# One transformer block on one core: a hand-written order of all operations replaced by another order of the same operations

## The chip, the cores and the metric

The kernel runs on one core of one Trainium2 chip. The metric is the device time of one execution in microseconds, the median over several runs. The core has five engines that run side by side, each of them through its own list of instructions in a fixed order: TensorE (PE), VectorE (DVE), ScalarE (ACT), GpSimd (POOL) and SyncE (SP). SP does no arithmetic here. It issues nearly all DMA transfers, one after the other; ACT issues the first two. An engine whose next instruction is not ready waits, and everything behind that instruction on the same engine waits with it.

## The reference: what is computed

A conditioning vector `c` gives shifts, scales and gates through `silu(c) @ w_mod`, six blocks of 512. A layer norm of x, scaled and shifted by the first two blocks, goes through sliding dilated attention; its output, multiplied by the third block, is added to x. A second layer norm, scaled and shifted by the next two blocks, goes through a gated GELU network; its output, multiplied by the sixth block, is added again. S is 2048, the width 512, there are 32 heads of 16, the window holds 8 keys at distances 0, 2, ... 14, and the hidden width is 1792. The two cores of it:

```python
idx = pos[:, None] - off[None, :]          # off = arange(8) * 2
logits = jnp.einsum('bhsd,bhswd->bhsw', q, kg) * scale
logits = jnp.where(mask[None, None, :, :], logits, -1000000000.0)
attn = _softmax(logits, axis=-1)
o = jnp.einsum('bhsw,bhswd->bhsd', attn, vg)
...
g = jnp.einsum('bsd,df->bsf', x, w_gate)
u = jnp.einsum('bsd,df->bsf', x, w_up)
h = _gelu(g) * u                            # then h @ w_down
```

## The kernel before, in words

The sequence is cut into four groups of 512 positions, each of four chunks of 128. Every step of the kernel is an `Op` with the engine that it goes to, a function that emits its instructions, the names of the ops that must come first, and the name that it fires when it is emitted. The ops stand in 123 generators, here called threads. Each thread gives its ops in a fixed order of its own: one thread for the matmuls of the query, key and value projection of group 0, one for the VectorE products of group 0, and so on. 26 such threads serve each group; others serve the loads, the conditioning vector, the warming up of TensorE and the scaling of the weights.

The order in which the threads are interleaved is written out by hand, as a list of thread numbers called `ORDER` at the top of the file:

```python
def run(self):
    nxt = [next(g, None) for g in self.threads]
    for i in ORDER:
        op = nxt[i]
        ...
        op.fn()
        ...
        nxt[i] = next(self.threads[i], None)
```

So `ORDER` alone decides which instruction stands behind which on each engine. The numbers that an `Op` carries as its duration are not used for anything when the kernel is built.

The threads that matter for the change, with the names of their ops and the lines that issue instructions (a trailing number is the group, then the head block or chunk):

- Warming up (thread 10): 15 matmuls on zeros, L202. They compute nothing that is used.
- Conditioning (thread 9): the activation `s4` of `c` on ACT (L315), its transposition `scp` on PE (L320), a copy back (`scT`, L324), a tiny exponential whose purpose is its table load (`pre`, L326), and two products with `w_mod`, `mp1` and `mp0` (L286), whose evictions give scale and shift of the first norm (L294, L291). Each of these products waits for its own 512 KB load, `wm1` and `wm0` (L223).
- Norms: statistics on DVE (`st`, L395; `ag`, L401), or on ACT for some chunks (`sa`, L378; `sq`, L384); the variance made ready (`vd`, L415, from DVE; `va`, L420, from ACT); the power -0.5 on POOL (`rs`, L426); the normalised chunks `x0` to `x3` on DVE (L435). LN1.g is the first norm of group g, LN2.g the second. LN1.0 is done in two halves of two chunks. Then come transposes, on PE (`th0` and `th1` at L472 for LN1.0, L449 for LN1.1, LN1.2 and LN2.0) or by DMA (L455), and the evictions with scale and shift (L487 on ACT; for LN1.0 L505 on ACT and L503 on DVE).
- Projections (`qp`, L536 and L554), evicted by ACT (L568, L570, L572).
- Attention of a group: `pq` multiplies queries with shifted keys on DVE (four ops, L617); `lp` sums over the head width on PE (L631); softmax on DVE and ACT (L643 to L675), for groups 2 and 3 behind a tiny exponential (`pre.2`, `pre.3`, L682) that loads its table; the probabilities go to memory and come back replicated (`est`, L687, and `pt`, L694, on SP); the values go to memory (`vst`, L591) and come back shifted (`V4`, four loads, L599); `pv` multiplies on DVE (four ops, L706); `o` sums on PE (L720); `oT` evicts on ACT (L731); `x1p` is the output projection (L741), and `x1` adds it to x on DVE (L750).
- Network of a group: 14 pairs of gate and up products on PE (`g` and `u`, L771), GELU and copy on ACT (`gl`, L803; `ub`, L810), their product on DVE (`hh`, L821), the down projection on PE (`y`, L783; `yl`, L794 for the very last chunk), the sum with x on DVE (`ot`, L828; L835 for the last) and the stores (L843, L852).
- Gates: the third block of the conditioning scales the weights `wo` on DVE (`woS`, L361), the sixth the weights of the down projection, in seven pieces (`WdS0` to `WdS6`, L356). Both need the gate spread over all partitions in one tile `gB`. That goes through memory: a store of 1 KB (`gst`, L298) and a load that replicates it (`ga` for `woS`, `gb` for `WdS`, L303). Blocks four and five pass through memory too (L305). The weights of the down projection come in four loads (`Wd0` to `Wd3`, L243). `Wd0` uses the buffer of the value weights again, so it has to wait until the last value projection of group 3 has read them.

SP's order is therefore part of `ORDER` too: a transfer that must wait there holds all transfers listed behind it.

Of the kernel before, what the change touches and what calls it, by code (L numbers as in the profile page):

```python
# [18 lines left out]
    1, 26, 2, 10, 0, 10, 2, 1, 2, 0, 2, 10, 10, 2, 10, 0, 10, 9, 10, 2, 9, 20, 9, 10, 20, 10, 18, 20, 10, 21,  # L19
    10, 18, 20, 10, 20, 2, 21, 20, 21, 10, 21, 10, 10, 21, 20, 20, 2, 9, 9, 9, 9, 21, 22, 9, 21, 10, 17, 23, 22,  # L20
    17, 3, 23, 24, 17, 24, 24, 11, 17, 23, 24, 17, 24, 24, 24, 44, 46, 2, 24, 24, 2, 46, 25, 25, 2, 46, 46, 24,
    25, 2, 46, 46, 44, 24, 2, 46, 25, 46, 24, 46, 25, 28, 24, 25, 4, 3, 24, 25, 70, 46, 24, 72, 70, 46, 24, 25,
    46, 46, 25, 28, 48, 25, 24, 49, 48, 49, 24, 49, 28, 49, 11, 29, 25, 29, 25, 50, 72, 27, 27, 11, 96, 5, 50,
    28, 96, 3, 50, 70, 51, 29, 70, 27, 72, 52, 72, 29, 98, 96, 27, 72, 30, 50, 51, 30, 5, 96, 50, 72, 51, 30,
    72, 51, 50, 51, 72, 30, 50, 98, 72, 72, 72, 96, 12, 13, 30, 74, 12, 51, 6, 50, 96, 98, 53, 30, 53, 50, 51,
    98, 51, 75, 30, 98, 50, 74, 75, 54, 31, 50, 27, 13, 75, 7, 50, 75, 51, 98, 78, 31, 55, 51, 98, 31, 76, 98,
    98, 54, 100, 76, 77, 76, 77, 76, 77, 16, 76, 4, 27, 77, 4, 32, 76, 4, 77, 6, 76, 77, 4, 51, 76, 4, 32, 77,
    4, 101, 76, 77, 76, 101, 32, 101, 33, 77, 33, 55, 101, 76, 77, 32, 51, 102, 77, 34, 76, 34, 7, 33, 54, 79,
    79, 4, 53, 33, 34, 4, 103, 102, 53, 34, 53, 102, 54, 53, 35, 35, 36, 55, 55, 36, 19, 7, 35, 56, 6, 19, 104,
    35, 19, 36, 77, 103, 102, 36, 37, 19, 102, 37, 103, 37, 102, 37, 103, 37, 37, 102, 56, 103, 37, 103, 102,  # L30
    103, 37, 56, 37, 102, 37, 37, 103, 56, 14, 103, 38, 14, 102, 39, 56, 38, 39, 102, 56, 39, 102, 39, 80, 57,
    103, 40, 4, 103, 8, 103, 40, 80, 40, 57, 57, 41, 40, 41, 40, 8, 41, 42, 41, 4, 40, 4, 41, 42, 4, 105, 40,
# [872 lines left out]
```

## Time and profile before

| | |
|---|---|
| median of three runs | 236.47 us (236.15 to 236.91) |
| span of the profiled execution | 234.1 us |
| TensorE busy | 228.9 us, 98% of the span |
| VectorE busy | 167.5 us, 72% |
| ScalarE busy | 148.4 us, 63% |
| GpSimd busy | 24.7 us, 11% |
| DMA moved | 30.42 MB |

The span runs from the first to the last instruction of the profiled execution. The runs are 2.4 us longer than that span, which is work outside the kernel's own instructions. Times within the profile are microseconds from the start of the span. Row heads read: start, length, engine, line, operation, output and inputs; "x8" means that eight instructions stand in one row; what stands in square brackets is the time that the engine sat idle ahead of the row and what released it. PE rows whose pieces overlap the next row are normal, since the ends of pipelined matmuls are modelled.

### The profile page before, as it was taken

How to read it: one execution, taken by the hardware profiler on the slowest of the kernel's cores; microseconds unless marked ns; L12 is line 12 of the kernel's file. 1: busy time of each engine (PE TensorE's matmuls, PEld its weight loads, DVE VectorE, ACT ScalarE, POOL GpSimd, SP SyncE). 2: the span in 40 equal slices, each digit the busy share in tenths (PEclk: the TensorE clock that was granted, in tenths of full speed). 3: DMA queues.
4: the chain of work that ended last, by engine and by line, in shares of the span. 5: the costliest groups of instructions: out<-in, count | busy, mean ns of one | idle time of the engine just before them, and what ended most of it. 6: DMA issues, size and time to landing. Idle time of an engine off the chain costs nothing.

```text
span 234.1 us, 3657 instructions
## 1 busy us (share of the span) xinstructions
PE 228.9 (98%) x1382; PEld 107.2 (46%) x1382; DVE 167.5 (72%) x240; ACT 148.4 (63%) x282; POOL 24.7 (11%) x37
## 2 busy tenths in 40 slices
PE   7899999999999999999999999999999999999995
PEld 2755454444544444444444444444444444444443
DVE  4889999999998999989999989916642122123222
ACT  4999996968995749928556961563568721466400
POOL 3210230892100000100000010000100000000000
PEclk9999999999999999999999999999999999999999
DMA  6998869999368280054404634100071001000011
GB/s 214 385 332 295 244 224 221 301 329 408 159 188 235 97 276 3 1 115 134 114 0 128 243 91 97 40 0 22 0 71 45 0 22 42 6 0 1 21 48 45
DMA packets 30313, 30.42 MB, mean 130 GB/s; under 512 B 14936, under 2 KB 26200, under 8 KB 30296
## 3 DMA queue, kind: packets, MB, share of 16 engines
q1 hardware_dynamic: 29760, 29.67, 41.3%
q10 hardware_dynamic: 536, 0.53, 0.6%
q8 instruction: 11, 0.18, 0.3%
q14 instruction: 6, 0.05, 0.1%
HBM read 22.78 MB, written 5.31 MB: 120 GB/s over the span
## 4 chain that ended last, share of the span: by engine, by line
PE 84%; DVE 9%; DMA 3%; ACT 1%; SPq 1%; issue 0%
PE g_ps L771 21%; PE u_ps L771 21%; PE y_ps L783 19%; PE qkv_ps L554 9%; PE x_ps L741 6%; DVE pq L617 5%; PE o_ps L720 3%; DMA x<-in_A_x_dram 3%; PE LTp L631 2%; PE y_ps L794 1%; DVE xn L435 1%; DVE st L395 1%; ACT qT L568 1%; DVE mx L648 1%; DVE LTp L654 1%; DVE e L675 1%
## 5 line engine op out<-in xcount | busy, mean ns | idle before, releaser
L771 PE MATMUL g_ps<-h,Wg 128*128 128x512 bf16 x224 | 57.5, 379 | 0.0
L771 PE MATMUL u_ps<-h,Wu 128*128 128x512 bf16 x224 | 57.5, 379 | 0.0
L803 ACT ACTIVATE gl<-g_ps 128x512 bf16<-128x512 f32 x56 | 33.8, 605 | 24.3 <-PE g_ps L771 23.4
L783 PE MATMUL y_ps<-Wd,hht 128*128 128x512 bf16 x210 | 47.0, 379 | 0.0
L821 DVE TENSOR_TENSOR hht<-gl,ub 128x512 bf16<-128x512 bf16 x56 | 23.2, 420 | 31.8 <-ACT ub L810 31.6
L810 ACT CAST ub<-u_ps 128x512 bf16<-128x512 f32 x56 | 33.0, 592 | 17.1 <-PE u_ps L771 17.1
L554 PE MATMUL qkv_ps<-hT,wqkv 128*128 128x512 bf16 x184 | 42.0, 380 | 0.2 <-ACT gR L349 0.2
L617 DVE TENSOR_TENSOR pq<-qT,kT 128x4096 bf16<-128x4096 bf16 x16 | 36.3, 2284 | 0.3 <-ACT kT L570 0.3
L706 DVE TENSOR_TENSOR pv<-PT,V 128x4096 bf16<-128x4096 bf16 x16 | 36.0, 2285 | 0.2 <-PE LTp L631 0.2
L771 PEld LDWEIGHTS <-Wg 128*128 128x128 bf16 x224 | 21.7, 98 | 27.2 <-issue 1.7
L771 PEld LDWEIGHTS <-Wu 128*128 128x128 bf16 x224 | 21.8, 98 | 26.8 <-issue 0.8
L783 PEld LDWEIGHTS <-hht 128*128 128x128 bf16 x210 | 20.4, 98 | 25.2 <-issue 0.8
L554 PEld LDWEIGHTS <-wqkv 128*128 128x128 bf16 x184 | 20.2, 114 | 18.8 <-issue 2.4
L426 POOL TENSOR_TENSOR rstd<-rstd,neghalf 128x4 f32<-128x4 f32 (+1 forms) x9 | 8.7, 971 | 122.3 <-DVE rstd L415 68.7
L828 DVE TENSOR_TENSOR ot<-y_ps,x 128x512 bf16<-128x512 f32 x15 | 10.2, 686 | 15.9 <-PE y_ps L783 15.9
L750 DVE TENSOR_TENSOR x<-x_ps,x 128x512 bf16<-128x512 f32 x16 | 10.8, 684 | 7.1 <-PE x_ps L741 7.1
L741 PE MATMUL x_ps<-woP,oT 128*128 128x512 bf16 x64 | 15.3, 379 | 0.0
L395 DVE BATCH_NORM_STATS2 st<-x 128x6 f32<-128x512 bf16 x19 | 12.5, 678 | 2.5 <-DMA x<-in_A_x_dram 2.5
L487 ACT ACTIVATE h<-h,modT,scl 128x512 bf16<-128x512 bf16 x12 | 9.0, 808 | 8.1 <-DMA h<-xn 8.1
L587 POOL COPY vh<-vT 128x64 bf16<-128x64 bf16 x3 | 12.0, 3992 | 16.7 <-ACT vT L572 16.7
L731 ACT CAST oT<-o_ps 128x512 bf16<-128x512 f32 x16 | 9.2, 600 | 6.6 <-PE o_ps L720 6.6
L378 ACT ACTIVATE gl<-x 128x512 bf16<-128x512 bf16 x13 | 8.3, 650 | 6.8 <-DVE x L750 6.0
(77 smaller groups left out, 186.8 us busy)
## 6 DMA issues: line engine op xcount, KB each, us to landing
V<-vscr SPq DMA_DIRECT2D x16, 526.0 KB, 6.7
wm<-in_w_mod_dram SPq DMA_DIRECT2D x5, 512.0 KB, 8.5
vscr<-vT SPq DMA_DIRECT2D x4, 528.0 KB, 7.4
out_dram<-ot SPq DMA_DIRECT2D x15, 128.0 KB, 1.7
Wg<-in_B_w_gate_dram SPq DMA_DIRECT2D x4, 448.0 KB
Wu<-in_B_w_up_dram SPq DMA_DIRECT2D x4, 448.0 KB, 7.6
wqkv<-in_A_wqkv_dram SPq DMA_DIRECT2D x3, 512.0 KB, 7.1
x<-in_A_x_dram SPq DMA_DIRECT2D x3, 512.0 KB, 8.0
```

The source lines that it names most:

```text
L395: nc.vector.bn_stats(out=k["st", c4][:], in_=src()[:, c4, :])
L554: nc.tensor.matmul(ps[:], lhsT=wqkv[blk][:, dt, j::4], rhs=B["hT", sg][:, :, dt, :], start=(dt == 0), stop=(dt == DT - 1))
L587: yield Op("POOL", 0.2, lambda: nc.gpsimd.tensor_copy(out=vh[:], in_=B["vT", sg][:, :, SG:VR]), after=[f"qkv.{sg}.2.3"], fire=f"vh.{sg}")
L617: nc.vector.tensor_tensor(out=pq[:], in0=_ap(B["qT", sg][:, j, :], [[0, W], [1, SG]]), in1=_ap(kT[:, j, sg * SG + 2:sg * SG + 2 + SG], [[2 ...
L706: nc.vector.tensor_tensor(out=t[:], in0=_ap(B["PT", sg][:, 0, :], [[SG, 2], [0, 4], [1, SG]]), in1=_ap(v[:, j, 0, :], [[8, 2], [VR, 4], [1 ...
L741: nc.tensor.matmul(ps[:], lhsT=B["oT", sg][:, j, c4 * P:(c4 + 1) * P], rhs=woP[:, j, :], start=(j == 0), stop=(j == 3))
L750: nc.vector.tensor_tensor(out=x[:, c4, :], in0=B["x1ps", sg, c4][:], in1=x[:, c4, :], op=ALU.add)
L771: nc.tensor.matmul(ps[:], lhsT=Wt[:, dt, ft * P:(ft + 1) * P], rhs=B["h2T", sg][:, :, dt, :], start=(dt == 0), stop=(dt == DT - 1))
L783: nc.tensor.matmul(ps[:], lhsT=B["hh", sg, ft][:, c4 * P:(c4 + 1) * P], rhs=B["Wd", ft // 4][:, ft % 4, :], start=(ft == 0), stop=(ft == F ...
L803: nc.scalar.activation(out=gl[:], in_=B["g", sg, ft][:], func=ACT.Gelu_apprx_tanh)
L810: nc.scalar.copy(out=ub[:], in_=B["u", sg, ft][:])
L821: nc.vector.tensor_tensor(out=hh[:], in0=B["gl", sg, ft][:], in1=B["ub", sg, ft][:], op=ALU.mult)
```

## The change

Only `ORDER` changes. The ops, their functions, buffers, shapes and data are the same, and so is the order within each thread. The whole list is replaced; its numbers tell a reader little. Its first line, for instance (10 is the warming up, 26 the zeroing of a margin, 2 the loads on SP, 20 the statistics of group 0):

```diff
 ORDER = [
-    1, 26, 2, 10, 0, 10, 2, 1, 2, 0, 2, 10, 10, 2, 10, 0, 10, 9, 10, 2, 9, 20, 9, 10, 20, 10, 18, 20, 10, 21,
+    10, 1, 2, 1, 20, 9, 0, 10, 20, 10, 9, 2, 2, 20, 20, 21, 10, 10, 10, 21, 9, 10, 2, 21, 9, 18, 20, 0, 20, 10,
...
```

On TensorE the start changes like this. Before, six warming matmuls stand ahead of `scp`, eight behind it, then `mp1`, `mp0`, `th0`, one more warming matmul and `th1`. Now two stand ahead of `scp`, seven behind it, then `mp1`, five more, `mp0`, `th0`, one more and `th1`. On VectorE, the variance of the first half of LN1.0 (`vd0`) moves behind the statistics of the second half.

**ScalarE, at the start, between the copy of the conditioning vector and the evictions of its products (gl is a scratch output, sums the statistic).** Before:

```order
L324 COPY scT<-scp 128x4
L378 ACTIVATE gl,sums<-x 128x512
L384 ACTIVATE gl,sums<-x,sums 128x512
L326 ACT_TABLE_LOAD
L326 ACTIVATE junk<-neghalf 128x4
L294 ACTIVATE scl<-modT_ps 128x4
```

After:

```order
L324 COPY scT<-scp 128x4
L326 ACT_TABLE_LOAD
L326 ACTIVATE junk<-neghalf 128x4
L378 ACTIVATE gl,sums<-x 128x512
L384 ACTIVATE gl,sums<-x,sums 128x512
L294 ACTIVATE scl<-modT_ps 128x4
```

The table load for the exponential moved ahead of the two statistics passes over chunk 3 of group 0.

**VectorE, at the first norm of group 1, once its statistics are made (pq are the products of queries and keys of group 0).** Before:

```order
L415 TENSOR_SCALAR rstd<-mv 128x3
L420 TENSOR_SCALAR rstd<-sums 128x1
L617 TENSOR_TENSOR pq<-qT,kT 128x4096
L435 TENSOR_SCALAR xn<-x,mv,rstd 128x512
L395 BN_STATS st<-x 128x6
L435 TENSOR_SCALAR xn<-x,mv,rstd 128x512 x2
L435 TENSOR_SCALAR xn<-x,sums,rstd 128x512
L617 TENSOR_TENSOR pq<-qT,kT 128x4096 x2
```

After:

```order
L415 TENSOR_SCALAR rstd<-mv 128x3
L420 TENSOR_SCALAR rstd<-sums 128x1
L435 TENSOR_SCALAR xn<-x,mv,rstd 128x512 x3
L395 BN_STATS st<-x 128x6
L435 TENSOR_SCALAR xn<-x,sums,rstd 128x512
L395 BN_STATS st<-x 128x6
L617 TENSOR_TENSOR pq<-qT,kT 128x4096 x4
```

The normalised chunks of group 1 moved ahead of the first product of group 0, so that nothing stands between `va` and them any more.

**SyncE, where the gate of the down projection is made and the probabilities of group 1 go through memory (V are the shifted values of group 1, Wd the down weights, escr and PT the probabilities).** Before:

```order
L599 DMA V_884<-vscr_109 128x1x2104 x3
L687 DMA escr_117<-e 128x1024
L243 DMA Wd_1099<-in_B_w_down_dram 128x4x512
L298 DMA gscr_115<-gR 4x128
L694 DMA PT<-escr_117 128x4x128 x2
L303 DMA gB<-gscr_115 128x512
L243 DMA Wd_1140<-in_B_w_down_dram 128x4x512
```

After:

```order
L305 DMA modc<-gscr_114 128x4x1
L243 DMA Wd_1106<-in_B_w_down_dram 128x4x512
L298 DMA gscr_115<-gR 4x128
L599 DMA V_1109<-vscr_109 128x1x2104
L303 DMA gB<-gscr_115 128x512
L687 DMA escr_117<-e 128x1024
L694 DMA PT<-escr_117 128x4x128 x2
```

`Wd0`, `gst5` and `gb` moved ahead of the store of the probabilities, and the first shifted load of the values of group 1 stands between them. On VectorE the scaling `WdS0` of the first piece moved with them. Before, it stands behind all four `pv` of group 1; now it stands directly behind the first of the `pq` of group 2, ahead of the second, of the first `hh` and of all `pv` of group 1.

Further on, the table load ahead of the softmax of group 3 (`pre.3`) now stands between a GELU and a copy of group 1, and the sums, projections and products of groups 2 and 3 interleave differently with the network's matmuls. All steps and counts stay, but for the ACT table loads, which the order of the functions decides: there are nine of them instead of seven.

66 rows, old and new, of the table ORDER are left out of this document.

## The prediction, made before the changed kernel was timed

> **What bounds the kernel now.** I read the page first, then busy time by stage, the groups of TensorE, the chain that ended last, and the timeline of the places that the change touches. From the page:
>
> ```profile
> span 234.1 us, 3657 instructions
> ...
> PE 84%; DVE 9%; DMA 3%; ACT 1%; SPq 1%; issue 0%
> ```
>
> The chain is TensorE for 84%, VectorE for 9%. The next view has busy time by stage, in the order PE, PEld, DVE, ACT, POOL, then clock, DMA share and GB/s:
>
> ```profile
> 36.00:66.00 30.00, 30.00 (x208) 14.93 (x205) 29.70 (x31) 24.52 (x48) 12.81 (x5) 1.00 0.82 274
> 66.00:97.00 31.00, 31.00 (x191) 13.36 (x189) 29.32 (x33) 23.47 (x50) 0.00 (x0) 1.00 0.48 147
> 97.00:230.00 133.00, 133.00 (x691) 59.61 (x688) 76.69 (x120) 68.53 (x114) 3.13 (x3) 1.00 0.21 55
> ```
>
> PE is never free in any of the three. Until 97 us DVE is full as well (29.70 of 30.00, 29.32 of 31.00), and DVE feeds PE there. Behind 97 DVE is busy for 77 of 133 us, so only the order could make PE wait.
>
> How much waiting is left for a better order to remove? A busy PE row may hide small waits, so I add up the work: groups of TensorE by line (count | busy, mean ns | idle ahead), then three pieces of the chain.
>
> ```profile
> L771 PE MATMUL g_ps<-h,Wg 128*128 128x512 bf16 x224 | 57.5, 379 | 0.0
> L771 PE MATMUL u_ps<-h,Wu 128*128 128x512 bf16 x224 | 57.5, 379 | 0.0
> L783 PE MATMUL y_ps<-Wd,hht 128*128 128x512 bf16 x210 | 47.0, 379 | 0.0
> L554 PE MATMUL qkv_ps<-hT,wqkv 128*128 128x512 bf16 x184 | 42.0, 380 | 0.2 <-ACT gR L349 0.2
> L741 PE MATMUL x_ps<-woP,oT 128*128 128x512 bf16 x64 | 15.3, 379 | 0.0
> L631 PE MATMUL LTp<-pq,Mph 128*32 128x512 bf16 x128 | 9.1, 381 | 0.2 <-DVE pq L617 0.2
> L720 PE MATMUL o_ps<-pv,Mph 128*32 128x512 bf16 x128 | 8.7, 381 | 0.0
> ```
>
> ```profile
> 44.80 0.98 PE o_ps L720 x16
> ...
> 219.10 9.06 PE y_ps L783 x42
> 228.17 3.07 PE y_ps L794 x28
> ```
>
> The mean of 379 ns is the length of one pipelined matmul; its rate is 9.06 / 42 = 0.2157 us. The 906 matmuls of the first five rows take 906 x 0.2157 = 195.4. The 256 of the next two take 256 / 16 x 0.98 = 15.7. The last chunk takes 3.1. For the transposes and small products behind the first projection I allow about 4, and 1.8 for the sixteen half-wide matmuls of that projection. Sum 220. PE works from 8.88 (row below) to 228.17 + 3.07 = 231.2, which is 222.3 us. So roughly 1.5 to 2.5 us of waiting, most of it likely the change from one kind of matmul to another, is all that a new order can take out behind 8.88, in 234. The tail (last matmul, sum, store: 2.9 us) stands as it was. Two waits are named, together 0.36:
>
> ```profile
> 24.93 0.61 PE L631 MATMUL LTp<-pq,Mph 128*32 128x512 bf16 x8 [0.15 <-DVE pq L617]
> ...
> 30.44 2.75 PE L554 MATMUL qkv_ps<-hT,wqkv 128*128 128x512 bf16 x12 [0.21 <-ACT gR L349]
> ```
>
> **The change part by part.** The sum is made against the profiled span of 234.1; the median of the runs, 236.47, is 2.37 above it, and I carry that 2.37 over. A difference below 0.3%, 0.7 us, can't be told from no change in a measurement of this kernel.
>
> *The head.* All later work stands behind the first projection, L536. Its chain, PE first, then the other engines:
>
> ```profile
> 1.25 2.74 PE L202 MATMUL warm_ps<-gB 128*128 128x512 bf16 x6 [1.25 <-DVE gB L197]
> 3.92 0.18 PE L320 MATMUL scp<-ident,c 4*128 4x4 bf16 x1
> 4.03 2.25 PE L202 MATMUL warm_ps<-gB 128*128 128x512 bf16 x8
> ...
> 7.28 0.55 PE L286 MATMUL modT_ps<-scT,wm 128*128 128x1 bf16 x16 [0.62 <-DMA wm<-in_w_mod_dram]
> ...
> 8.36 0.61 PE L472 MATMUL hTp<-ident,xn 128*128 128x128 bf16 x8
> 8.88 0.38 PE L536 MATMUL qkv_ps<-hT,wqkv 128*128 128x256 bf16 x2
> ```
>
> ```profile
> 3.14 0.31 ACT L315 ACTIVATE c<-c 4x128 bf16<-4x128 bf16 x1
> ...
> 4.84 0.63 ACT L378 ACTIVATE gl<-x 128x512 bf16<-128x512 bf16 x1 [0.54 <-DMA x<-in_A_x_dram]
> ...
> 6.43 1.28 ACT L326 ACT_TABLE_LOAD   x1
> ```
>
> ```profile
> 5.99 1.52 POOL L426 TENSOR_TENSOR rstd<-rstd,neghalf 128x2 f32<-128x2 f32 x2 [3.26 <-DVE mv L401]
> ...
> 7.88 0.41 DVE L435 TENSOR_SCALAR xn<-x,sums,rstd 128x512 bf16<-128x512 bf16 x1
> ```
>
> Two things get later. First, ACT: the table load of 1.28 now runs ahead of L378. The copy `scT` follows `scp`, which is ready at 3.14 + 0.31 = 3.45, so the load runs from about 3.9 to 5.2 and L378 starts at 5.3, not at 4.84: the variance `va` and with it the second power on POOL move by 0.47. On POOL the two powers take 0.76 each. The first starts 0.25 later, since `vd0` moved behind other DVE steps, and the second now waits for `va`, about 7.07. It ends at about 7.85 and not 7.51; the last normalised chunk ends near 8.7 in place of 8.29, `th1` starts near 8.77, and L536 at about 9.2, 0.33 later. The load cost nothing where it stood, since ACT had no work for the head then; its cover is gone.
>
> Second, the clock. At full rate a warming matmul takes 0.216. The first six took 2.74, about 0.43 each and a drain. The eight behind `scp` took 2.25: with the same drain of 0.17, 1.6 of them at 0.43 and the rest at 0.216. So the full clock came at about 4.7, 3.5 us after the first matmul at 1.25, with PE idle for almost none of it. In the new order PE has two warming matmuls (1.25 to 2.1), then waits for `c` until 3.45: 1.35 us of idle time in that stretch. If the clock still comes at 4.7, seven matmuls end near 5.7, `mp1` near 6.1 and the next five at 7.3 to 7.4, about when `wm0` lands (7.28): nothing is lost beyond the 0.33. If it comes 3.5 us after the unbroken run starts at 3.66, at 7.2, the seven end at 6.65, `mp1` at 7.2, and the five fast ones hold `mp0` until 8.3: `th0` waits, and L536 stands about 1.0 later than before. The Trainium skill, page "TensorE: Matmul & The Clock Gate", section "Part 1: The HAM clock gate", says that the clock is opened after a window of about 3.4 us that was busy, and that this window runs freely, so that the number of slow matmuls differs by run. The trace agrees with the size (3.5 here); by that rule the gap could cost a whole window, which the third rival takes up, and no run here shows yet how much idle time a window stands. I take 0.6 for the head, nearer to the first end (ends 0.33 and 1.0).
>
> *LN1.1.* Timeline, POOL then DVE:
>
> ```profile
> 13.26 1.01 POOL L426 TENSOR_TENSOR rstd<-rstd,neghalf 128x4 f32<-128x4 f32 x1 [5.74 <-DVE rstd L420]
> ...
> 13.02 0.15 DVE L420 TENSOR_SCALAR rstd<-sums 128x1 f32<-128x1 f32 x1 [0.55 <-ACT gl L384]
> 13.50 2.29 DVE L617 TENSOR_TENSOR pq<-qT,kT 128x4096 bf16<-128x4096 bf16 x1 [0.32 <-ACT kT L570]
> ```
>
> Before, POOL's 1.01 lay beside the 2.29 of `pq.0.0`. Now the normalised chunks stand directly behind `va`, so DVE waits for the power: 1.01 and the two handovers, about 1.17. It waited 0.55 + 0.32 = 0.87 there before, of which the 0.32 goes (the key is evicted meanwhile). Queued behind this wait are all four `pq.0` and with them everything of group 0. Net +0.2 to +0.3. What comes back: the transposes of LN1.1 are ready 3 us earlier, so PE has projections of group 1 to do while it waits for `lp.0`, and the two named waits of 0.36 may go.
>
> *DVE to 66 us.* DVE has some 0.3 us free of 30, so its lateness stays. The head 0.3 to 0.6, LN1.1 0.2, and about 0.2 around the maximum of group 0, which stands earlier in the row and waits for `lp.0`: 0.7 to 1.0 at the end of LN2.0.
>
> ```profile
> 60.51 0.73 DVE L435 TENSOR_SCALAR xn<-x,mv,rstd 128x512 bf16<-128x512 bf16 x2
> ...
> 61.74 0.62 PE L449 MATMUL hTp<-ident,xn 128*128 128x128 bf16 x8
> ...
> 65.23 1.03 PE L771 MATMUL g_ps<-h,Wg 128*128 128x512 bf16 x4
> ```
>
> LN2.0 ends at 61.24 and its transposition starts at 61.74: about 0.4 of slack. What goes beyond it moves the whole network: +0.3 to +0.6, and I take 0.5. This isn't on top of the head; the head's lateness reaches the end by this road or by PE's own, whichever is later.
>
> *The gate of the down projection.* Rows: `gb` from issue to landing, its neighbours on SP, and the DVE row ahead of the new place of `WdS0`.
>
> ```profile
> DMA to landing us min/median/max: 4.8/5.6/6.3
> ```
>
> ```profile
> 65.24 0.39 SPq L243 DMA_DIRECT2D Wd<-in_B_w_down_dram  x1
> 65.72 0.55 SPq L298 DMA_DIRECT2D gscr<-gR  x1
> ...
> 68.71 0.33 SPq L303 DMA_DIRECT2D gB<-gscr  x1
> ```
>
> ```profile
> 64.70 4.48 DVE L617 TENSOR_TENSOR pq<-qT,kT 128x4096 bf16<-128x4096 bf16 x2
> ```
>
> `Wd0` needs the value weights' buffer, whose last reader in the new order runs at about 59.3 (three projections of 0.86 ahead of 61.4, and the lateness). So `Wd0` goes out at 59.35, `gst5` at 59.85, and `gb` 2.99 behind it as before (68.71 less 65.72), at about 62.8. It lands at 67.6 with the shortest landing, at 68.4 with the median, at 69.1 with the longest. DVE reaches `WdS0` after one `pq` of 2.24: 64.70 + 2.24 + 0.5 = 67.45. What is queued behind a waiting `WdS0`: `pq.2.1`, `hh.0.0`, then all of `pv.1`, whose sums PE needs in its row; about 0.8 us of slack lie on that way. So the wait costs PE 0 (landing up to 68.2) to 0.9 (69.1). Median landing: 0.2; I take 0.3, since `V4.1.0` stands between `gst5` and `gb` and two more loads share the queue. If `gb` came earlier than 67.45 it would cost nothing, and no gain is possible, as PE is fed at that place already.
>
> *The store of the probabilities* of group 1 goes out behind `gb`, not ahead of it; it is ready at 65, after `gb` at 62.8: nothing. *Values of group 0 and 1*: the shifted loads stand later on SP and took 4.6 to 9.8 from issue to landing.
>
> ```profile
> DMA to landing us min/median/max: 4.6/6.7/9.8
> ```
>
> `pv.0.3` runs near 47.6 and its load goes out at 42.3: it fits at the shortest, not at the median (1.4 late), but the waiting is shared with `WdS0` and PE has projections there. I take 0 (ends 0 and 1.0). *Two more table loads on ACT* (nine for seven), 2 x 1.28, between 117 and 130 us: ACT is busy for 68.53 of 133 us there and PE has four buffers ahead, so 0 (ends 0 and 0.5). *Everything later*: moves of `lp`, `x1p`, `ot` among the 133 us with PE full; the small rest of waits there, about 0.4, may shrink, and I give it 0.
>
> Sum: 0.5 for head and DVE chain to the network, 0.3 for the gate: +0.8, so 236.47 + 0.8 = 237.3.
>
> **The rivals.** *The forecast*: 0.5 to 1.6 later, 237.1 to 238.1.
>
> *No change*: the clock comes at 4.7 as before, the landing of `gb` is median or shorter, and the waits that the new order removes pay for the head: +0.3 at the network, +0.1 for the gate, -0.4 of late waits: 236.5. For it: PE has 1.5 to 2.5 us that aren't work. Against: most of that is switching between kinds of matmul, and both orders hold 15 runs of the summing matmuls.
>
> *Faster*: PE's early projections decide, not DVE. With the transposes of LN1.1 3 us earlier, PE always has projections ready, the waits before 66 us go, about 1.0, and LN2.0 is later by no more than its slack of 0.4. It decides if DVE's lateness at LN2.0 stays below 0.4: then the network starts up to 0.4 earlier, the other 0.4 goes later: -0.8, 235.7. For it: the two named waits are both of that kind. Against: LN2.0 hangs on DVE, which is full, and the wait for the power is new.
>
> *Much slower*: the idle 1.35 us makes the clock miss its time until 8.2, one more 3.5 us interval behind 4.7. Then all warming matmuls and `mp0` run at half rate, `mp0` ends past 8.7 and L536 starts at 10.3, 1.4 later, which goes to the end nearly whole; with the longest landing of `gb`, 0.9: +2.3, 238.8. For it: an idle stretch this long within the first 3.5 us is nowhere in the trace of before. Against: PE is busy for two thirds of that time.
>
> **How the numbers follow.** Forecast 0.39, no change 0.36, faster 0.17, much slower 0.08. So slower by over 0.3%: 0.39 + 0.08 = 0.47; within 0.3%: 0.36; faster: 0.17. The time is that of the likeliest, 237.3. Its own range is 237.1 to 238.1; the range that holds the time 8 times in 10 takes in the faster case at its lower end and most of the much slower one: 235.6 to 238.9.
>
> **What would show it.** Right: L378 at 5.3, a warming matmul at 0.43 still behind 4.7 or not, L536 past 9.1, an idle of about 1.1 on DVE ahead of the L435 rows of LN1.1, L771 starting at 65.5 to 65.9, and DVE waiting at L356 for `gb` near 67.5. Wrong: L771 starting at 65.2 or earlier, or `gb` landed before DVE comes; then the waits ahead of PE in the new trace tell whether it is the faster rival. A network that starts late while the end isn't late would mean that the rest behind 66 us was larger than my 0.4.

## The result, and the profile after

The changed kernel takes 239.49 us (median of four runs, 238.40 to 240.95) against 236.31 for the kernel before in the same comparison: a ratio of 1.0127, with an interval from 1.0084 to 1.0170. Run a second time, it came out at 240.11 against 236.62: 1.0143 (1.0114 to 1.0172). So it is slower by 3.2 to 3.5 us. I had forecast slower, but by 0.8. Medians are over all executions of a kernel; the ratios leave out single executions that took over 1.5% longer than the kernel's fastest, and three traces below come from such executions (a_v 271.6 us, b_same 244.15, a_m 243.37), so nothing is argued from the first two and little from the third.

One thing about the sizes first. The profiled execution of the changed kernel took 238.40 with a span of 236.7, so 1.7 us lie around the span. So the work around the span is 1.7, not the 2.4 given with the profile before: the span before, 234.1, with the same 1.7 makes 235.8, less than any of the three runs shown with it. That execution was shorter than the median, and so is the one profiled now (the fastest of its four). The two traces differ by 2.6 us and the medians by 3.2.

From the page of the changed kernel:

```profile
span 236.7 us, 3659 instructions
...
PE 86%; ACT 7%; DMA 3%; SPq 2%; ACTq 0%; issue 0%; DVE 0%
```

VectorE, 9% of this chain before, has no share in it now. Followed back, the chain runs along TensorE to a wait of 0.26 for the load of the sixth conditioning block (the row at 56.47 below) and so leaves VectorE's waits aside. It names the last wait, not what the change costs; the run a_m below moves that product away.

Busy time by stage, same columns as before:

```profile
36.00:66.00 30.00, 28.48 (x202) 13.73 (x200) 28.18 (x28) 22.96 (x46) 1.81 (x5) 1.00 0.74 212
66.00:97.00 31.00, 31.00 (x181) 13.54 (x183) 30.63 (x32) 22.78 (x45) 0.00 (x0) 1.00 0.50 160
```

The stage from 36 to 66 us has changed. TensorE, without a gap there before, is now free for 1.52 us of 30, and VectorE is busy for 28.18, not 29.70. TensorE's three waits there:

```profile
46.80 0.62 PE L720 MATMUL o_ps<-pv,Mph 128*32 128x512 bf16 x8 [0.60 <-DVE pv L706]
...
50.08 1.89 PE L554 MATMUL qkv_ps<-hT,wqkv 128*128 128x512 bf16 x8 [0.57 <-ACT kT L570]
...
56.47 0.41 PE L344 MATMUL gR_ps<-wm,scB 128*32 128x128 bf16 x16 [0.26 <-DMA wm<-in_w_mod_dram]
```

Behind this stage nothing is lost. The last piece of the chain is

```profile
230.72 3.07 PE y_ps L794 x28
```

so from the first network matmul (67.64, below) to the end of the last it takes 166.15 us, against 166.01 before (65.23 to 231.24).

The head, TensorE's timeline:

```profile
3.50 0.18 PE L320 MATMUL scp<-ident,c 4*128 4x4 bf16 x1 [1.23 <-ACT c L315]
3.61 3.17 PE L202 MATMUL warm_ps<-gB 128*128 128x512 bf16 x7
...
7.04 1.24 PE L202 MATMUL warm_ps<-gB 128*128 128x512 bf16 x5
...
9.71 1.91 PE L536 MATMUL qkv_ps<-hT,wqkv 128*128 128x256 bf16 x16
```

Seven warming matmuls stand in 3.17, all at 0.43; five in 1.24, all at 0.216. So the full clock came at 6.6 to 7.0, not at 4.7, and the first projection starts 0.83 later.

VectorE's timeline shows where the rest arises; from the statistics of LN1.1 to the network these are all rows with a wait in brackets.

```profile
14.38 1.06 DVE L435 TENSOR_SCALAR xn<-x,mv,rstd 128x512 bf16<-128x512 bf16 x3 [1.13 <-POOL rstd L426]
...
29.67 0.17 DVE L420 TENSOR_SCALAR rstd<-sums 128x3 f32<-128x3 f32 x1 [0.22 <-ACT gl L384]
...
42.25 6.70 DVE L706 TENSOR_TENSOR pv<-PT,V 128x4096 bf16<-128x4096 bf16 x3 [1.10 <-DMA PT<-escr]
49.50 2.29 DVE L706 TENSOR_TENSOR pv<-PT,V 128x4096 bf16<-128x4096 bf16 x1 [0.55 <-DMA V<-vscr]
```

The same place in the kernel before has all four products in one row, without a wait:

```profile
39.91 8.89 DVE L706 TENSOR_TENSOR pv<-PT,V 128x4096 bf16<-128x4096 bf16 x4
```

The wait for the power (1.13) was in the prediction; the 1.10 for the probabilities and the 0.55 for the fourth shifted load were not. Together they are most of VectorE's lateness: the statistics of LN1.1 start 0.73 late, the power costs 0.26 more than the 0.87 before, and with 0.22, 1.10 and 0.55 that makes 2.86; the last chunks of LN2.0 start 2.85 later (63.36, not 60.51).

Why both arrive late is read on SyncE. The kernel before, from the store of the probabilities on:

```profile
33.19 0.33 SPq L687 DMA_DIRECT2D escr<-e  x1
33.56 0.54 SPq L599 DMA_DIRECT2D V<-vscr  x1
...
35.18 0.92 SPq L694 DMA_DIRECT2D PT<-escr  x2
36.72 3.06 SPq L455 DMA_TRANSPOSE hT<-xn  x1
...
40.45 0.55 SPq L599 DMA_DIRECT2D V<-vscr  x1
```

The changed kernel:

```profile
35.32 0.32 SPq L687 DMA_DIRECT2D escr<-e  x1
...
37.58 0.93 SPq L694 DMA_DIRECT2D PT<-escr  x2
38.55 0.53 SPq L599 DMA_DIRECT2D V<-vscr  x1
39.19 4.88 SPq L455 DMA_TRANSPOSE hT<-xn  x1
...
44.78 0.56 SPq L599 DMA_DIRECT2D V<-vscr  x1
```

The store of the probabilities goes out 2.1 later (35.32, not 33.19) and their loads 2.4 later (37.58, not 35.18). The third shifted load, 526 KB, now stands directly ahead of the transposition of LN1.3. That transposition holds SyncE for 4.88 in place of 3.06, and the fourth load, behind it, goes out at 44.78 in place of 40.45. The profile puts the time within the transposition down to TensorE's projections. They can't be what it waits for: it uses the buffer of LN1.1's transposed chunks again, and the last projection that reads those ended at 36.0, before the transposition was begun at 39.19.

Further on, TensorE, VectorE and SyncE around the network's start and the gate:

```profile
67.64 1.03 PE L771 MATMUL g_ps<-h,Wg 128*128 128x512 bf16 x4
```

```profile
67.55 2.28 DVE L617 TENSOR_TENSOR pq<-qT,kT 128x4096 bf16<-128x4096 bf16 x1
69.75 0.69 DVE L356 TENSOR_TENSOR Wd<-Wd,gB 128x1024 bf16<-128x1024 bf16 x1
```

```profile
65.21 0.33 SPq L303 DMA_DIRECT2D gB<-gscr  x1
```

The network starts at 67.64, 2.40 later. `WdS0` follows the product without an idle time: VectorE came to it 2.3 later than I had reckoned, and the gate was there, although its load too went out 2.4 later than I had reckoned (65.21, not 62.8).

### The profile page after: what moved, and what is told of

It is laid out like the page before. It is cut to its first block, busy times and chain, and to the rows that moved or that the text cites. A ratio compares the mean times of both kernels' runs of the same rounds, so it can differ in the third digit from the quotient of the medians.

```text
span 236.7 us, 3659 instructions
## 1 busy us (share of the span) xinstructions
PE 229.7 (97%) x1382; PEld 107.2 (45%) x1382; DVE 167.6 (71%) x240; ACT 151.6 (64%) x284; POOL 16.0 (7%) x37
## 4 chain that ended last, share of the span: by engine, by line
PE 86%; ACT 7%; DMA 3%; SPq 2%; ACTq 0%; issue 0%; DVE 0%
PE g_ps L771 21%; PE u_ps L771 21%; PE y_ps L783 19%; PE qkv_ps L554 10%; PE x_ps L741 5%; DMA wm<-in_w_mod_dram 3%; PE o_ps L720 2%; PE warm_ps L202 2%; PE LTp L631 2%; ACT gl L384 1%; ACT gl L378 1%; PE y_ps L794 1%; ACT vT L572 1%; SPq L208 1%; ACT hT L487 1%; PE hTp L449 1%
## 5 line engine op out<-in xcount | busy, mean ns | idle before, releaser
L771 PE MATMUL u_ps<-h,Wu 128*128 128x512 bf16 x224 | 57.6, 380 | 0.0
L771 PE MATMUL g_ps<-h,Wg 128*128 128x512 bf16 x224 | 57.5, 379 | 0.0
L554 PE MATMUL qkv_ps<-hT,wqkv 128*128 128x512 bf16 x184 | 42.3, 380 | 0.7 <-ACT kT L570 0.6
L771 PEld LDWEIGHTS <-Wg 128*128 128x128 bf16 x224 | 21.7, 98 | 27.1 <-issue 1.5
L771 PEld LDWEIGHTS <-Wu 128*128 128x128 bf16 x224 | 21.6, 98 | 27.2 <-issue 1.7
L741 PE MATMUL x_ps<-woP,oT 128*128 128x512 bf16 x64 | 15.9, 380 | 0.0
L570 ACT CAST kT<-qkv_ps 128x512 bf16<-128x512 f32 x16 | 10.0, 627 | 1.3 <-PE qkv_ps L554 1.3
L568 ACT CAST qT<-qkv_ps 128x512 bf16<-128x512 f32 x16 | 9.7, 613 | 1.5 <-PE qkv_ps L554 0.8
```

The source lines that it names most:

```text
L554: nc.tensor.matmul(ps[:], lhsT=wqkv[blk][:, dt, j::4], rhs=B["hT", sg][:, :, dt, :], start=(dt == 0), stop=(dt == DT - 1))
L741: nc.tensor.matmul(ps[:], lhsT=B["oT", sg][:, j, c4 * P:(c4 + 1) * P], rhs=woP[:, j, :], start=(j == 0), stop=(j == 3))
L771: nc.tensor.matmul(ps[:], lhsT=Wt[:, dt, ft * P:(ft + 1) * P], rhs=B["h2T", sg][:, :, dt, :], start=(dt == 0), stop=(dt == DT - 1))
```

## The experiments

Edits are shown as orders of ops on one engine. All times below are medians, each ratio is against the kernel before on the same chip; an interval of 0.3 to 0.5% on each side is what these measurements give, so single steps of under 0.5% are seen only by their sum or by the trace.

Heads differ by execution, as will be seen, so here is for each trace the stretch from the first statistics of LN1.1 on VectorE to the first network matmul, and what VectorE was idle within it (the sum of the idle times in brackets on its rows):

| kernel | statistics | first L771 | stretch | VectorE idle |
|---|---|---|---|---|
| before | 10.11 | 65.23 | 55.1 | 0.87 |
| changed | 10.84 | 67.64 | 56.8 | 3.00 |
| changed, again (a_same) | 11.90 | 70.10 | 58.2 | 4.34 |
| a_x | 11.32 | 67.11 | 55.8 | 1.75 |
| a_xv | 11.43 | 71.28 | 59.9 | 5.80 |
| a_head | 10.73 | 69.09 | 58.4 | 4.63 |
| a_xh | 10.73 | 68.45 | 57.7 | 3.79 |
| a_s | 10.92 | 66.62 | 55.7 | 2.02 |
| a_m | 14.24 | 72.37 | 58.1 | 4.40 |
| a_xsm | 13.81 | 68.75 | 54.9 | 1.36 |
| a_xsmh | 11.71 | 68.66 | 57.0 | 3.14 |
| a_xsmhl | 10.16 | 66.72 | 56.6 | 3.00 |
| b_warm | 10.80 | 66.01 | 55.2 | 0.97 |
| b_l11 | 12.58 | 69.05 | 56.5 | 2.22 |
| b_sp | 11.12 | 67.98 | 56.9 | 2.87 |

The stretch less the idle time is 53.6 to 54.3 in all fifteen, while the stretch itself goes from 54.9 to 59.9. Less TensorE's idle time it is 54.8 to 57.0, which fits less closely. So what VectorE idles on this way is what the way takes longer, whatever the edit; that bears out the theory called A below. It takes out the start of the execution, which was especially late in a_xsm and a_m, but not all of what differs between executions: the waits themselves vary.

**The changed kernel again (a_same).** No edit.

> The changed kernel once more, nothing edited, to see how far its runs differ and what in the trace differs with them. Theory A (VectorE's chain): the network starts when the second norm of group 0 ends on VectorE, and what VectorE idles on the way there sets the time: head 0.73 later, 0.26 more for the power of LN1.1, 0.22 for statistics, 1.10 for the probabilities, 0.55 for the fourth shifted load, in all 2.84 less 0.4 of slack; it expects about 239.5 and those idle times again within 0.3. Theory B (TensorE's own waits): TensorE loses its 2.5 us between 44 and 57 us because the projections of group 3 wait for the transposed LN1.3 and for key evictions; same time. Theory C (clock): the late clock of the head is the loss and differs by run: a run with a first projection later than 9.7 is later at the end by as much.

240.11 against 236.62, 1.0143 (1.0114 to 1.0172). Its head:

```profile
3.62 3.17 PE L202 MATMUL warm_ps<-gB 128*128 128x512 bf16 x7
...
7.05 2.29 PE L202 MATMUL warm_ps<-gB 128*128 128x512 bf16 x5
...
10.76 1.47 PE L536 MATMUL qkv_ps<-hT,wqkv 128*128 128x256 bf16 x12
```

Five warming matmuls in 2.29: all slow. The same program got its full clock 2 us later than in the first trace, and its first projection stands at 10.76. Theory C is right that the head differs by run. But the stretch behind the head is longer here too, 58.2, so the head is not the whole of it. VectorE idled 1.63 for the probabilities and 1.08 for the fourth load, 0.5 more for each than in the first trace, where theory A had allowed 0.3: those waits vary as well.

**LN1.3 back (a_x).**

```diff
 VectorE, changed kernel
-LN1.3.x0, s1.0, LN1.3.x1, ri.0, LN1.3.x2, p.0, pq.1.0, LN1.3.x3
+s1.0, ri.0, p.0, pq.1.0, LN1.3.x0, LN1.3.x1, LN1.3.x2, LN1.3.x3
```

> The changed kernel, with the normalised chunks 0 to 2 of LN1.3 back behind the first product of group 1 on VectorE, ahead of chunk 3, as in the kernel before. The probabilities go out 0.97 earlier. Theory A: VectorE's idle 1.10 ahead of the first pv falls to about 0.1, but the fourth shifted load still lands at 49.4, so the idle time ahead of pv.0.3 grows from 0.55 to about 1.5: the network starts as late as now, 239.4, no change over 0.3. If each wait had a price of its own: 1.0 faster, 238.5. Theory B: the transposed LN1.3 comes no earlier, no change, 239.5. Theory C: no change.

238.77, ratio 1.0084 (1.0054 to 1.0114), 1.3 us better than the changed kernel beside it. Theory A as I put it, that the fourth load would take over the whole wait, isn't borne out by this trace: neither wait is left in it, and the stretch is 55.8. But it depends on the execution. In the trace of a_xh, which has the same edit, the wait for the probabilities is gone and the fourth load does take over:

```profile
49.69 2.29 DVE L706 TENSOR_TENSOR pv<-PT,V 128x4096 bf16<-128x4096 bf16 x1 [1.84 <-DMA V<-vscr]
```

The normalised chunks, 1 us of VectorE's time, had been moved ahead of the probabilities. That is not neutral on a full engine. Behind the store of the probabilities they cover the way through memory; ahead of it they delay its start. How much of the delay is handed on isn't simple: with the edit the store goes out at 35.05, and, measured from the statistics of LN1.1, that is 0.75 earlier than in the changed kernel. The loads behind it go out no earlier (38.03; from the statistics 26.71, with 26.74 in the changed kernel). They only landed sooner, and the transposition held SyncE for 3.69, not 4.88.

**Shifted loads ahead (a_v, a_xv).**

```diff
 SyncE, changed kernel
-est.0, Wg.3, pt.0.0, pt.0.1, V4.0.2, LN1.3.t, gst4, V4.0.3
+est.0, Wg.3, V4.0.2, V4.0.3, pt.0.0, pt.0.1, LN1.3.t, gst4
```

> The changed kernel, with the third and fourth shifted loads of the values of group 0 moved on SyncE from behind the probabilities (and, the fourth, from behind the transposition by DMA) to ahead of the probabilities' loads, where SyncE waits for the store anyway. Theory A: the idle 0.55 ahead of pv.0.3 goes, the 1.10 ahead of pv.0.0 stays: 0.5 faster, 239.0. Theory B: the transposition by DMA goes out 0.6 earlier and the projections of group 3 with it: 0.6 faster or a little more, 238.9. Theory C: no change.

> The changed kernel with both edits: normalised chunks 0 to 2 of LN1.3 back behind the first product of group 1, and the third and fourth shifted loads ahead of the probabilities' loads. Theory A: both idle times on VectorE go, 1.10 and 0.55: 1.5 to 1.65 faster, 237.9, and the first L771 row at about 66.0 in place of 67.6. Theory B: as with the loads alone, 0.6 faster, 238.9. Theory C: no change, 239.5.

Both missed, on the wrong side: a_v 242.68, 1.0232 (1.0192 to 1.0272); a_xv 241.81, 1.0174 (1.0124 to 1.0225). VectorE in the trace of a_xv:

```profile
45.69 4.49 DVE L706 TENSOR_TENSOR pv<-PT,V 128x4096 bf16<-128x4096 bf16 x2 [2.84 <-DMA PT<-escr]
```

The wait for the probabilities is 2.84, with 1.10 in the changed kernel and none in a_x's trace. Their issue alone moved to 40.64, from 38.03 in a_x. They wait for the store of the probabilities, issued at 36.05, which needs 4.59 now in place of 2.98, with two loads of 526 KB behind it on the queue. No theory had this: I had counted issue slots on SyncE, not what the data on the queue takes.

**TensorE's head (a_head, a_xh, b_warm).**

```diff
 TensorE, changed kernel (a_head, a_xh); b_warm is the reverse, in the kernel before
-warm x2, scp, warm x7, mp1, warm x5, mp0, th0, warm, th1
+warm x6, scp, warm x8, mp1, mp0, th0, warm, th1
```

a_xh has the edit of a_x as well.

> The changed kernel with TensorE's own order of the kernel before up to the second transposition of LN1.0: six warming matmuls ahead of the transposed conditioning vector, eight behind it, none between the two products; everything else as changed. The traces so far have the full clock granted at 4.78 us in the kernel before, and at about 6.8, 9.2, 8.0 and 6.3 with the changed head, and the first projection at 8.89 against 9.7 to 10.8. Theory A (VectorE's chain passes the head's lateness on): clock back at about 4.8, first projection at 9.2 since the table load stays early, the end 0.5 to 1.5 earlier: 239.0 beside 240.1. Theory D (TensorE catches up between 9 and 36 us and the head costs nothing): no change, 240.1.

> The changed kernel with two edits: TensorE's head as before, and the normalised chunks 0 to 2 of LN1.3 back behind the first product of group 1, which alone gave 238.8 beside 240.1. Theory A: the two add up, 1.3 and 1.0: 237.7, with VectorE idle only ahead of LN1.1 (1.1) and near 0.2 for statistics. Theory B (TensorE's waits between 44 and 57 us stay, whatever VectorE does): 238.6.

> The kernel before with only TensorE's head of the changed one: two warming matmuls ahead of the transposed vector, seven behind it, five between the two products. The table load stays where it was. Theory A: clock at 6.3 to 9.2 instead of 4.8, first projection 0.4 to 1.7 later, and VectorE, which is full up to the second norm, hands on all but 0.4 of it: 0.3 to 1.3 slower, 237.4 beside 236.6. Theory D (TensorE catches up): 236.6.

a_head 239.75, 1.0110 (1.0066 to 1.0155); a_xh 238.84, 1.0077 (1.0050 to 1.0104); b_warm 237.16, 1.0019 (0.9986 to 1.0052). By their ratios each differs by 0.1 to 0.4% in the direction expected, 0.2 to 0.8 us, from the kernel that it starts from (a_xh from a_x); none is clear of no change by itself. The 237.7 that theory A had for a_xh, a_x and the head added up, missed: 238.84 is theory B's number. Its trace shows waits of both kinds, 1.84 on VectorE for the fourth load and 2.4 on TensorE in four places, so it doesn't tell the two theories apart; the table above does, for VectorE. In b_warm's trace the first projection is 0.8 later, the network 0.8 later, the stretch 55.2: what the head loses in this execution goes on to the network, against theory D. But heads in the order of before can be late too: in a_head's trace the clock came early and the first projection still stood at 9.57, as `mp0` waited 0.99 for its load (for the clock see b_same below). So the medians differ by less than two single traces.

**LN1.1 ahead (b_l11).**

```diff
 VectorE, kernel before
-LN1.1.va0, pq.0.0, LN1.1.x0, LN1.2.st0, LN1.1.x1, LN1.1.x2, LN1.1.x3
+LN1.1.va0, LN1.1.x0, LN1.1.x1, LN1.1.x2, LN1.1.x3, pq.0.0, LN1.2.st0
```

> The kernel before with the four normalised chunks of LN1.1 ahead of the first product of group 0, as in the changed kernel. VectorE waits about 1.1 for the power instead of 0.87. Theory A: 0.25 later on VectorE, within the 0.4 of slack at the second norm: no change over 0.3, 236.7. Theory E (the earlier transposes let TensorE run ahead and that reaches the end): 0.4 to 0.9 faster, 235.9.

237.35, 1.0023 (0.9994 to 1.0052). Not faster by the 0.4 to 0.9 us of theory E, which falls; whether it costs 0 or 0.5% can't be told.

**SyncE's order as before (a_s), and the small product (a_m).**

```diff
 SyncE, changed kernel (a_s)
-V4.0.0, ga, gst3, Wg.2, vst.1, V4.0.1, est.0, Wg.3, pt.0.0, pt.0.1, V4.0.2, LN1.3.t, gst4, V4.0.3
+V4.0.0, V4.0.1, ga, gst3, Wg.2, vst.1, est.0, V4.0.2, pt.0.0, pt.0.1, LN1.3.t, gst4, V4.0.3, Wg.3
 TensorE, changed kernel (a_m)
-lp.1.2, mp5, lp.1
+lp.1.2, lp.1, mp5
```

> The changed kernel with SyncE's order around the probabilities of group 0 as in the kernel before: the second shifted load of the values behind the first, the third behind the store of the probabilities, the fourth behind the transposition by DMA, and the last piece of the gate weights behind that. In four traces of the changed order the third shifted load stands directly ahead of the transposition of LN1.3: the transposition held SyncE for 3.7 to 5.0 us and landed 5.7 to 7.1 after its issue, against 3.06 and 4.57 in the kernel before; behind it the fourth load went out late. Theory F (SyncE's order): the transposition lands after 4.6, the probabilities after 3.5, the fourth load is early; VectorE's idle 1.10 to 1.8 ahead of pv.0.0 and 0.55 to 1.1 ahead of pv.0.3 go: 1.5 faster than the changed kernel, 238.4. Theory G (the probabilities are late because they are made late, VectorE's order): 0.5 faster at most, 239.5.

> The changed kernel with the small product of the sixth conditioning block on TensorE moved from ahead of the last sum of logits of group 1 to directly behind it. In five traces TensorE waited there for that block's load, 0.26, 0.97, 0.50, 1.81 and 1.28, with the sum of logits, and behind it the maximum on VectorE, queued behind. Theory H (the small product holds the sum up): 0.3 to 1.4 faster, 239.3. Theory A (VectorE is late by then for other reasons, and takes up the wait): 0 to 0.3 faster, 239.9.

a_s 238.17, 1.0064 (1.0031 to 1.0096), so 1.5 to 1.9 us better than the changed kernel, as theory F had it. VectorE and SyncE in its trace:

```profile
41.13 8.94 DVE L706 TENSOR_TENSOR pv<-PT,V 128x4096 bf16<-128x4096 bf16 x4
```

```profile
37.38 0.92 SPq L694 DMA_DIRECT2D PT<-escr  x2
38.40 3.18 SPq L455 DMA_TRANSPOSE hT<-xn  x1
...
42.30 0.54 SPq L599 DMA_DIRECT2D V<-vscr  x1
```

All four products in one row again, although the probabilities still went out late (37.38 against 35.18): the transposition holds SyncE for 3.18, and the fourth load is in time. Theory G falls. Note that this edit moves a third transfer as well, the last piece of the gate weights (`Wg.3`), from ahead of the probabilities to behind the fourth load. a_m 240.61, 1.0133 (1.0088 to 1.0178): no gain is seen, though the interval just takes in theory H's 239.3. TensorE's waits at the small product, as the expectation lists them, were there, but theory H isn't borne out in the changed kernel: with the product moved, VectorE still idles 4.40 in a_m's trace, 2.42 of it for the probabilities. With SyncE's order mended the product does reach VectorE: in a_s's trace its maximum waits 0.68 for the sum of logits, in a_xsm's, where the product is moved, not at all.

**Together (a_xsm, a_xsmh, a_xsmhl).** First the edits of a_x, a_s and a_m; then the whole head as before; then, besides, `pq.0.0` back ahead of the chunks of LN1.1.

```diff
 ScalarE and VectorE, a_xsmh, beside TensorE's head
-scT, pre, LN1.0.sa3, LN1.0.sq3, mod1
+scT, LN1.0.sa3, LN1.0.sq3, pre, mod1
-LN1.0.st2, LN1.0.ag2, LN1.0.vd2, LN1.0.vd0
+LN1.0.st2, LN1.0.vd0, LN1.0.ag2, LN1.0.vd2
```

> The changed kernel with three edits: normalised chunks of LN1.3 back behind the first product of group 1, SyncE's order as before around the probabilities of group 0, and the small product behind the sum of logits. What stays of the change ahead of the network: the head, LN1.1, TensorE's order of projections. Theories A, F and H together: VectorE idles only for the head, LN1.1 and 0.2 for statistics; the first L771 row at about 66.3, the end at 237.4. If something else in the order between 36 and 66 us holds it: 238.5.

> As the last, and the whole head as before: TensorE's warming matmuls, ScalarE's table load behind the statistics, VectorE's variance. Theories A, F and H: first projection at 8.9 to 9.2, the end 0.3 to 0.8 earlier than without it, 236.9, about the kernel before; faster than the kernel before if TensorE's earlier projections are worth anything at the end (236.2).

> The changed kernel with all parts undone that were found to cost (LN1.3 on VectorE, SyncE's order around the probabilities, the head) and, besides, the first product of group 0 back ahead of the normalised chunks of LN1.1. What stays: TensorE's order of projections, the gate's early way, everything behind 66 us. Theory A: 0.1 to 0.3 faster than without the last edit, at most 0.2 from the kernel before: 236.8. If TensorE's order of projections is worth its early work: 0.5 to 0.9 faster than the kernel before, 236.1.

a_xsm 237.64, 1.0037 (1.0004 to 1.0070); a_xsmh 237.13, 1.0010 (0.9974 to 1.0046): with these parts undone, the kernel is back where it was, and the stretch of a_xsm, 54.9, isn't longer than that of before. a_xsmhl 237.94, 1.0036 (1.0002 to 1.0071), no better. Its trace shows why the last edit doesn't pay:

```profile
13.65 2.29 DVE L617 TENSOR_TENSOR pq<-qT,kT 128x4096 bf16<-128x4096 bf16 x1 [1.07 <-ACT kT L570]
...
24.32 2.29 DVE L617 TENSOR_TENSOR pq<-qT,kT 128x4096 bf16<-128x4096 bf16 x1 [1.50 <-ACT kT L570]
```

The products wait for keys. The keys are evicted in the changed ScalarE order, which, it seems, fits the products where the change has them. No version beat the kernel before.

**SyncE's order alone, in the kernel before (b_sp), and the kernel before again (b_same).**

```diff
 SyncE, kernel before (b_sp)
-V4.0.0, V4.0.1, ga, gst3, vst.1, est.0, V4.0.2, gst4, pt.0.0, pt.0.1, LN1.3.t
+V4.0.0, ga, gst3, vst.1, V4.0.1, est.0, gst4, pt.0.0, pt.0.1, V4.0.2, LN1.3.t
```

> The kernel before with two transfers moved on SyncE to where the changed kernel has them: the second shifted load of the values of group 0 behind the store of group 1's values, the third directly ahead of the transposition of LN1.3. Theory F1 (this order alone is the cost): the transposition lands 2 us later, the fourth load goes out 2 us later, and VectorE waits about 1 us ahead of pv.0.3: 0.7 to 1.2 slower, 237.8. Theory F2 (it costs only where the probabilities are late as well): probabilities and loads still land in time for VectorE, which reaches pv.0.0 at 39.9 and pv.0.3 at 46.5, waits of 0 to 0.4: no change over 0.4, 237.0 beside 236.8.

> The kernel before once more, with a trace of its own: does its head vary by run as the changed one's does? Theory C2 (the clock's window runs freely, and both heads meet it at any phase): the full clock between 4.1 and 7.5 instead of 4.8, the first projection between 8.9 and 9.6, and the stretch from the statistics of LN1.1 to the first L771 row within 0.3 of 55.1. Theory C3 (an unbroken run of warming matmuls gets the clock at 4.8 always): clock within 0.3 of 4.78.

b_sp 238.23, 1.0086 (1.0052 to 1.0119): two transfers moved, 1.5 us slower by the medians and 2.0 by the ratio. Theory F1, with more than its price. VectorE, then SyncE:

```profile
41.01 6.69 DVE L706 TENSOR_TENSOR pv<-PT,V 128x4096 bf16<-128x4096 bf16 x3
49.59 2.29 DVE L706 TENSOR_TENSOR pv<-PT,V 128x4096 bf16<-128x4096 bf16 x1 [1.90 <-DMA V<-vscr]
```

```profile
32.58 0.57 SPq L599 DMA_DIRECT2D V<-vscr  x1
34.29 0.32 SPq L687 DMA_DIRECT2D escr<-e  x1
...
38.17 0.92 SPq L694 DMA_DIRECT2D PT<-escr  x2
39.13 0.54 SPq L599 DMA_DIRECT2D V<-vscr  x1
39.79 3.58 SPq L455 DMA_TRANSPOSE hT<-xn  x1
44.03 0.55 SPq L599 DMA_DIRECT2D V<-vscr  x1
```

No wait for the probabilities here, though they are issued at 38.17; the fourth load at 44.03 alone costs VectorE 1.90. Measured from the statistics of LN1.1 it goes out 2.6 later than before, and the transposition's longer hold (3.58 against 3.06) is only 0.5 of that. The other 2.0 lie ahead of it: the store of the probabilities went out at the same time from the statistics, but their loads, which wait for it, 2.0 later.

Both effects can be followed through the traces. Where the second shifted load had gone out 8 us or more ahead of the store (before, a_s, a_xsm, a_xsmh, a_xsmhl, b_warm, b_l11), the loads of the probabilities follow the store by 1.99 to 2.00. Where it stands 1.7 to 2.9 ahead of it (the changed kernel, a_same, a_x, a_head, a_xh, a_m, b_sp), they follow by 2.15 to 3.88. And the transposition holds SyncE for 1.97 to 3.18 in the first seven, for 3.58 to 5.62 in the other seven, which have the third shifted load directly ahead of it. No run moved one of these two loads without the other, so what each is worth by itself in the time isn't shown.

b_same 236.78, 1.0011 (0.9976 to 1.0047). In its trace the clock (about 6.7) and the first projection (9.36) lie where theory C2 had them, and the stretch (56.6, with 55.1 expected within 0.3) does not; the granted clock over the whole of it was 0.95. For the head that trace isn't needed, since six others begin on TensorE in the same order, six warming matmuls, `scp`, eight warming matmuls. The eight, in b_sp and in a_xsmh:

```profile
4.03 2.09 PE L202 MATMUL warm_ps<-gB 128*128 128x512 bf16 x8
```

```profile
4.03 3.47 PE L202 MATMUL warm_ps<-gB 128*128 128x512 bf16 x8
```

The eight took 2.25 in the first trace of before, and 2.43 in a_head, 3.32 in a_xh, 3.07 in a_xsmhl, 2.66 in b_l11. With 0.43 for a slow one and 0.216 for a fast one, 2.09 has one slow one among the eight and 3.47 has nothing but slow ones: the full clock came at about 4.5 in the one and not before 7.0 in the other, in one and the same order. Both lie in theory C2's range, 4.1 to 7.5; theory C3 falls.

## Why the prediction was wrong, point by point

- *Where the bound lies.* Right. The end moves with the first network matmul, and that with VectorE, which is full up to there: the table of stretches shows it.
- *Behind 66 us.* Right: table loads, later sums and projections cost nothing (166.15 against 166.01 us).
- *Values of group 0.* This is the step that failed: "it fits at the shortest, not at the median (1.4 late), but the waiting is shared with `WdS0` and PE has projections there. I take 0". I let the fourth load go out at 42.3. It went out at 44.78, and 1.8 of these 2.5 us are the transposition ahead of it, which held SyncE for 4.88 with 3.06 in the row of before. The prediction has no term for what the 526 KB directly ahead would do to that, nor for what the second shifted load would do to the store of the probabilities. VectorE then waited 1.10 for the probabilities and 0.55 for the fourth load in the first trace, 1.63 and 1.08 in the second, and `WdS0`, which was to share it, did not wait. The same two moves in the kernel before cost 1.5 to 2.0 us (b_sp), and undoing them, together with the move of `Wg.3`, gave 1.5 to 1.9 back (a_s). My upper end for the step was 1.0.
- *LN1.3.* The prediction has no term for it at all. Three normalised chunks moved ahead of the probabilities, on an engine that I had called full; the work is the same, but the cover of a way through memory is gone. Undone alone: 1.3 us back (a_x). It overlaps with the loads. Either edit takes the wait for the probabilities away; that of LN1.3 left none for the fourth load in one trace and 1.84 in another. With both, nothing is left of the longer stretch (a_xsm, 54.9, against 55.1).
- *The head.* Right in kind. The ACT road came out as reckoned: L378 starts at 5.30, where I had 5.3. The clock came late, as at the worse end of the step, and the single trace shows 0.83 where I took 0.6, and another 1.9. Undoing it in the otherwise repaired kernel (a_xsm to a_xsmh) gave 0.5 us, within what the measurement tells.
- *LN1.1.* Right: VectorE waited 1.13 where I had 1.17.
- *DVE to 66 us.* 0.7 to 1.0 forecast at the end of LN2.0, 2.85 measured. The two waits that no term of the sum has make 1.65 of it, 1.10 and 0.55.
- *The gate.* I took 0.3; it cost nothing, because VectorE came later than the gate. A wait that I had priced was hidden by one that I had not.
- *The faster rival.* Half of its mechanism is there: the two named waits of TensorE are gone, and the first projections of group 2 start at 35.84, with 35.96 before, in spite of a head 0.8 later. It is worth nothing at the end, since VectorE decides.
- *Much slower.* Its 238.8 is near the measured time, but not by its own road, which was the clock and the longest landing of `gb`. The clock did come late, the gate cost nothing, and the waits that made the rest are not in it. That 238.8 is near is luck.
- *The direction.* It was forecast for reasons that hold as far as they go: the head and the wait for the power did make VectorE late. They are worth 1.0 of the 2.85.
- *What would show it.* L378 at 5.30, slow warming matmuls behind 4.7, L536 at 9.71 and 1.13 idle ahead of the rows of LN1.1 came as said. The network didn't: 67.64, where 65.5 to 65.9 was said. And VectorE did not wait for `gb`.
- *The range.* Its upper end, 238.9, rested on that rival. No rival and no term had VectorE waiting for a transfer ahead of 66 us, so the sum and the range were both short of it.

What stays open: how the wait for the probabilities in the changed kernel divides. Measured from the statistics of LN1.1, the second of their loads landed 2.3 later than before in the first traces. The store went out 1.4 later, its own way took 0.3 more, and the load's landing 0.6 more. But in a_x's trace the store was 0.75 earlier and the loads were not, so these parts don't simply add up. a_x and a_s each remove the wait.

## What to carry to other kernels

On an engine that is full, moving work past the start of a round trip through memory is not neutral: what stood behind the start covered the trip, ahead of it it delays the trip. So for each round trip list what moved from behind to ahead. On a DMA queue a big load a little ahead of a transfer that someone waits for can make that transfer slower (here 3.6 to 5.6 us of holding the queue in place of 2.0 to 3.2), and it delays everything behind it on the queue as well; a price for a transfer is read with its neighbours, not taken from a row with other neighbours. And one trace of a kernel isn't its price: the same edit left no wait in one trace and 1.84 us in another.

## What the runs showed of the hardware that I had not expected

The full clock of TensorE comes at different times in executions of one program. By the warming matmuls: before 7.05 in one trace of the changed kernel and behind 9.1 in the other, and from about 4.5 to past 7.0 in traces that begin in the order of before. The Trainium skill, page "TensorE: Matmul & The Clock Gate", section "Part 1: The HAM clock gate", says that the window behind it runs freely and that the number of slow matmuls varies by run; these traces agree.

It can be taken back as well. In a_xv, where TensorE waited for VectorE, busy time by stretch (the column behind POOL is the granted clock):

```profile
47.00:50.70 3.70, 1.51 (x24) 0.48 (x23) 3.70 (x3) 3.13 (x5) 0.00 (x0) 1.00 0.87 285
50.70:54.10 3.40, 3.40 (x12) 1.17 (x9) 3.40 (x2) 0.75 (x2) 0.00 (x0) 0.50 0.62 194
```

TensorE worked for 1.51 of 3.70 us, and the next 3.4 us ran at half the clock, although it was busy there throughout. So waits of 2.2 us on TensorE were followed by a loss of up to 1.7 more, half of 3.4 (an estimate from these two rows). It doesn't follow each time: in a_head's trace TensorE waits 1.16 and 1.81 us in this stage, and its clock stays full there.
